# Attention of a three-stage kernel: jobs ordered by a time table per quad of heads, VectorE's small results in a PSUM bank

## The chip, the cores and the metric

The program runs on one core of a Trainium2 chip, in one launch. The metric is the device time in microseconds. The engines are named as in the profile: PE is TensorE (PEld its weight loads), DVE VectorE, ACT ScalarE, POOL GpSimd, SP SyncE, which issues most of the DMAs here (SPq is its queue).

## The reference

Three stages follow each other. The first is attention with a window of 32 positions to either side plus 32 global tokens, for 4 batches of 8 heads of size 64 (512 local, 32 global positions). The second sends each of the 2304 tokens to the one expert out of 8 with the largest logit. The third is an MLP of width 2048.

```python
s_g = scale * np.matmul(q_g, k_all.transpose(0, 1, 3, 2))   # global queries see all 544 keys
out_g = np.matmul(sm(s_g), v_all)
...
mask = np.abs(pos[:, None] - pos[None, :]) <= window
s_ll = np.where(mask, s_ll, -1000000000.0)
s_l = np.concatenate([s_lg, s_ll], axis=-1)
out_l = np.matmul(sm(s_l), np.concatenate([v_g, v_l], axis=2))
...
expert_idx = np.argmax(x @ w_gate, axis=1)      # top-1 MoE, x: 2304 x 512
out[mask] = gate_w[mask, None] * (np.maximum(xe @ w1[e], 0.0) @ w2[e])
...
g = np.where(h >= 1, h, np.where(h <= -1, 0.0, (h + 1) ** 2 / 4))   # h = x @ w_in
return g @ w_out
```

## The kernel before

The 32 heads (4 batches of 8) are 16 **pairs** c, and two pairs are a **quad** q, so a batch is two quads. Each job of the attention is a function that writes its instructions on several engines at once; every engine then runs its own queue in the order in which the jobs were called. The jobs, with the short names that the texts use:

- **S** (`s_pair(c)`): scores of a pair, 64 small matmuls on PE (L253) and two mask matmuls for each head (L256) into two PSUM tiles `sp`.
- **M** (`s_max(n)`): per head, DVE takes the maximum over `sp` (L262, result `mx`, 128x4) and scales it (L263, `mn`). **E** (`s_exp(n)`): four exponentials on ACT (L280) from `sp` to `p`, with their sums.
- **T** (`t_head(n)`): per head, four transposes on PE (L335) into `ps_o`, which DVE copies to `pto` (L336).
- **P** (`pv(c)`): 64 matmuls of `pto` with the values (L380) into `xo`; DVE adds 1e-9 to the sums (L383), takes reciprocals (L384, `ri`) and scales `xo` to `xr` (L385). **V**: POOL spreads a value tile over the partitions in three copies (`spread_v`, L225 to L227), and SP issues the load of a later one (`load_v`).
- **X** (`x_turn`): transposes of `xr` on PE (L395), copied to `xT` by ACT (L396). **XS**: the store of `xr`. **K**: loads of a later pair's keys and queries.
- **G, GM, GE, GN, TG, PG**: the same steps for the 32 global queries of the four heads of a quad (L292; L303 to L305; L316; L322 to L324; L346; L356, whose results POOL copies into `xrg`, L362).
- **L, LT, R** per batch: the router's logits (L402), their transposes (L411), and `route`, nine steps on DVE (L457 to L466) with one exponential on ACT; after it `early` puts the rank matmuls on PE (L491 to L494, into the bank `gxb`), six DVE steps (`place`) and one-hot tiles on POOL.

A list, `units`, holds eight quads of five units (one global, four heads). A loop walks it and calls, at each unit, the jobs that are due at fixed lags: transposes two units after the scores (`LT`), the global transposes three after (`LG`). Jobs of the router go into the lists `tasks` and `fill`, from which the loop calls one task at each unit and up to `RATE` = 8 DVE steps in a row. The last jobs (from `t_head(30)` on) are written out by hand. All loads and stores go through `dma`, which lets a transfer start only when at most `ROOM` = 3.0 units (of 512 KB) are ahead of it on the SP queue.

PSUM has eight banks of 512 fp32 columns: tag "s" 3 (score tiles), tag "x" 1 (`xo`), tag "to" 3 (`ps_o`, `ps_x`, `lg`), and `gxb` alone. Columns 0 to 64 of `gxb` hold a part of the global scores, 128 to 192 the output of PG, 256 to 304 the ranks, 448 to 456 global logits. Where two engines use the same bank, the later one waits for the earlier, whichever columns each uses.

After the attention come the experts and the second MLP, large matmuls over blocks of gathered tokens; the change does not touch them.

## Time and profile before

| | |
|---|---|
| median of 3 runs (lowest, highest) | 740.49 us (738.86, 744.5) |
| profiled execution: its time, its span | 741.64 us, 739.8 us |
| PE busy | 711.3 us (96%), 6609 matmuls |
| DVE, ACT, POOL busy | 486.1 us (66%), 332.1 us (45%), 150.2 us (20%) |
| chain that ended last, by engine | PE 79%, issue 8%, DVE 7%, ACT 2%, DMA 2% |

The span runs from the first to the last instruction that the profiler saw; 1.84 us of the execution lie outside it. The page also cuts the span into 40 slices of 18.5 us and gives each a digit, the busy share of the engine in tenths. PE has 6889888 in the first seven slices, which are the attention, and 9 in every slice from there to the last but one.

### The profile page before, as it was taken

The numbers are of one execution on the slowest core, as the hardware profiler recorded it, in microseconds if no ns is written. First come the engines' busy times: TensorE is split into PE (matmuls) and PEld (weight loads), VectorE is DVE, ScalarE is ACT, GpSimd is POOL, SyncE is SP. The second block draws the span as 40 slices with busy tenths as digits, with TensorE's granted clock in tenths as the row PEclk, the third lists the DMA queues.
The fourth block names the chain that finished last, engine by engine and source line by source line (L and its number), as shares of the span: only waits on it lengthen the run. The fifth ranks groups of instructions, "written<-read, shape, count | busy, mean of one in ns | idle before, by whom it ended". The sixth has DMA issues, their size and how long they took to land.

```text
span 739.8 us, 16419 instructions
## 1 busy us (share of the span) xinstructions
PE 711.3 (96%) x6609; PEld 637.6 (86%) x6609; DVE 486.1 (66%) x887; ACT 332.1 (45%) x762; POOL 150.2 (20%) x185
## 2 busy tenths in 40 slices
PE   6889888999999999999999999999999999999995
PEld 4666666999999999899998898999989898998984
DVE  4778885674516478875777678758775876645443
ACT  4757664453525457664564543233323332322220
POOL 3445543677641340000000000000000000011112
PEclk9999999999999999999999999999999999999998
DMA  8786666485658578763531321101110100001111
GB/s 280 237 258 202 203 194 186 134 291 196 190 166 301 199 252 305 244 208 104 122 99 58 105 68 57 58 1 58 57 58 1 58 0 1 1 30 57 43 43 71
DMA packets 52254, 96.07 MB, mean 130 GB/s; under 512 B 9817, under 2 KB 27769, under 8 KB 50128
## 3 DMA queue, kind: packets, MB, share of 16 engines
q1 hardware_dynamic: 48704, 84.75, 36.1%
q0 software_dynamic: 3472, 10.25, 4.2%
q8 instruction: 53, 0.87, 0.5%
q14 instruction: 25, 0.20, 0.1%
HBM read 80.28 MB, written 14.75 MB: 128 GB/s over the span
## 4 chain that ended last, share of the span: by engine, by line
PE 79%; issue 8%; DVE 7%; ACT 2%; DMA 2%; POOL 1%; SPq 0%; POOLq 0%; ACTq 0%; DVEq 0%
PE fh L988 7%; PE fh L986 7%; PE fh L987 7%; PE o L988 6%; PE o L987 6%; PE o L986 6%; PE hp L988 4%; PE hp L986 4%; PE hp L987 4%; PE yp L986 4%; PE yp L987 4%; PE yp L988 4%; PE ps_o L335 2%; PE sp L253 2%; DMA ks<-in_k 2%
## 5 line engine op out<-in xcount | busy, mean ns | idle before, releaser
L1318 DVE SCALAR_TENSOR_TENSOR r<-r 128x384 f32<-128x384 f32 (+1 forms) x96 | 51.4, 535 | 113.4 <-ACT r L1317 113.4
L986 PE MATMUL o<-wh,gh 128*128 128x512 f32 x272 | 106.9, 393 | 0.8 <-ACT acc L1367 0.8
L988 PE MATMUL o<-wh,gl 128*128 128x512 f32 x272 | 107.6, 396 | 0.0
L987 PE MATMUL o<-wl,gh 128*128 128x512 f32 x272 | 107.3, 394 | 0.0
L1371 POOL DMA_INDIRECT out_dram<-acc,rid x17 | 16.5, 969 | 446.4 <-DVE acc L1369 444.8
L1320 ACT ACTIVATE gh<-g 128x384 fp32r<-128x384 f32 (+1 forms) x96 | 48.8, 508 | 129.2 <-DVE g L1319 129.2
L988 PE MATMUL fh<-yh,wl 128*128 128x384 f32 (+1 forms) x320 | 104.3, 326 | 0.0
L986 PE MATMUL fh<-yh,wh 128*128 128x384 f32 (+1 forms) x320 | 104.2, 326 | 0.0
L987 PE MATMUL fh<-yl,wh 128*128 128x384 f32 (+1 forms) x320 | 104.2, 326 | 0.0
L1317 ACT ACTIVATE r<-fh,half 128x384 f32<-128x384 f32 (+1 forms) x96 | 54.0, 562 | 105.6 <-PE fh L988 105.0
L986 PEld LDWEIGHTS fh<-yh,wh 128*128 128x128 f32 x320 | 60.2, 188 | 3.5
L987 PEld LDWEIGHTS fh<-yl,wh 128*128 128x128 f32 x320 | 60.2, 188 | 3.4
L988 PEld LDWEIGHTS o<-wh,gl 128*128 128x128 f32 x272 | 51.1, 188 | 12.4 <-DVE gl L1326 0.4
L988 PEld LDWEIGHTS fh<-yh,wl 128*128 128x128 f32 x320 | 60.2, 188 | 0.0
L986 PEld LDWEIGHTS o<-wh,gh 128*128 128x128 f32 x272 | 51.1, 188 | 9.1 <-ACT acc L1367 1.2
L987 PEld LDWEIGHTS o<-wl,gh 128*128 128x128 f32 x272 | 51.1, 188 | 8.1
L280 ACT ACTIVATE p<-sp,mn 128x128 f32<-128x128 f32 x128 | 45.2, 373 | 20.0 <-DVE mn L263 10.1
L1319 DVE TENSOR_TENSOR g<-r,fh 128x384 f32<-128x384 f32 (+1 forms) x96 | 51.0, 532 | 3.3
L986 PE MATMUL yp<-hTh,w2h 128*128 128x256 f32 (+5 forms) x176 | 51.7, 294 | 0.0
L988 PE MATMUL yp<-hTh,w2l 128*128 128x256 f32 (+5 forms) x176 | 51.2, 291 | 0.0
L987 PE MATMUL yp<-hTl,w2h 128*128 128x256 f32 (+5 forms) x176 | 51.1, 290 | 0.0
L1326 DVE TENSOR_TENSOR gl<-g,gh 128x384 fp32r<-128x384 f32 (+1 forms) x96 | 50.7, 529 | 0.0
(238 smaller groups left out, 1617.3 us busy)
## 6 DMA issues: line engine op xcount, KB each, us to landing
w1r<-in_w SPq DMA_DIRECT2D x32, 512.0 KB
w2r<-in_w SPq DMA_DIRECT2D x32, 512.0 KB
wraw<-in_wf SPq DMA_DIRECT2D x16, 1024.0 KB
ks<-in_k SPq DMA_DIRECT2D x16, 400.0 KB
v<-in_v SPq DMA_DIRECT2D x16, 384.0 KB
yr<-ys SPq DMA_DIRECT2D x68, 64.0 KB
qp<-in_q SPq DMA_DIRECT2D x16, 256.0 KB
xs<-xr SPq DMA_DIRECT2D x8, 512.0 KB
```

The costliest lines, as they stand in the source:

```text
L253: nc.tensor.matmul(sps[2 * c + z][a * WIN:(a + 1) * WIN, i, :], lhsT=q[r, j * WIN:(j + 1) * WIN], rhs=k_at(k, r, j), start=(i == 0), stop= ...
L280: nc.scalar.activation(p[:, i, :].rearrange("p (a b w) -> p a b w", a=2, b=2), v, AF.Exp, bias=mn[:, i:i + 1], scale=scale, accum_out=ss[b ...
L335: nc.tensor.transpose(o[:, i, :], p[:, i, :], ident)
L986: nc.tensor.matmul(o, lhsT=ah, rhs=bh, start=first, stop=False)
L987: nc.tensor.matmul(o, lhsT=ah, rhs=bl, start=False, stop=False)
L988: nc.tensor.matmul(o, lhsT=al, rhs=bh, start=False, stop=last)
L1317: nc.scalar.activation(r[:, 0:w], o[:, 0:w], AF.Relu, bias=half, scale=0.5)
L1318: nc.vector.scalar_tensor_tensor(r[:, 0:w], r[:, 0:w], 1.0, r[:, 0:w], ALU.min, ALU.mult)
L1319: nc.vector.tensor_tensor(g[:, 0:w], r[:, 0:w], o[:, 0:w], ALU.max)
L1320: nc.scalar.activation(gh[:, 0:w], g[:, 0:w], AF.Copy)
L1326: nc.vector.tensor_tensor(gl[:, 0:w], g[:, 0:w], gh[:, 0:w].bitcast(F32), ALU.subtract)
L1371: w = nc.gpsimd.indirect_dma_start(out=out, out_offset=bass.IndirectOffsetOnAxis(ap=rid[:, tt:tt + 1].bitcast(U32), axis=0), in_=a, in_off ...
```

## The change

**The order.** The loop with its lags goes. Each job has a time, in units of one quad: the quad's number plus a number from `TIMES` (one for each time that the job occurs in a quad) plus, for the global jobs of the first two quads, a number from `SHIFT`. All jobs are sorted by that time and called in that order. The jobs of the end that are in `LAST` are left to the part written out by hand, in which one transpose of `xr` is now called later and POOL's `weigh` as well.

**The small results.** `mx` (M), the sums plus 1e-9 (P), and for the first three batches the logits `L` and the scores `sc` (`route`) are no tiles in SBUF any more but columns 64 to 72, 72 to 80, 192 to 224 and 80 to 120 of `gxb`. The instructions are the same ones.

**The banks.** The bank of tag "x" goes to tag "s", which has 4; `xo` is taken from tag "to", which keeps 3.

**The start.** The load of `qg` (the queries of the global tokens) is issued ahead of the first values.

In the changed file the lines up to P's stand one lower (L262 is L261, L335 is L334); those of `route` are unchanged.

```diff
@@ -180,7 +180,7 @@
...
-    wps = ps.tile([128, 512], F32, tag="s", name="sp", bufs=3)
+    wps = ps.tile([128, 512], F32, tag="s", name="sp", bufs=4)
...
@@ -244,8 +244,7 @@
     def s_pair(c):
...
         for z in range(2):
-            home, n = ("x", 1) if c == 1 and z else ("s", 3)
-            sps[2 * c + z] = ps.tile([128, 4, BW], F32, tag=home, name="sp", bufs=n)
+            sps[2 * c + z] = ps.tile([128, 4, BW], F32, tag="s", name="sp", bufs=4)
...
@@ -257,7 +256,7 @@
 
     def s_max(n):
         sp = sps[n]
-        mx = ap.tile([128, 4], F32, tag="mx4", name="mx4", bufs=2)
+        mx = gxb[:, 64 + 4 * (n % 2):68 + 4 * (n % 2)]
         mn = ap.tile([128, 4], F32, tag="mn", name="mn", bufs=3)
         nc.vector.tensor_reduce(mx, sp, axis=AX.X, op=ALU.max)
         nc.vector.tensor_single_scalar(mn, mx, -scale, op=ALU.mult)
...
@@ -372,7 +371,7 @@
...
-        xo = ps.tile([128, 4, 2, D], F32, tag="s" if c == 15 else "x", name="xo", bufs=3 if c == 15 else 1)
+        xo = ps.tile([128, 4, 2, D], F32, tag="to", name="xo", bufs=3)
...
@@ -380,8 +379,9 @@
...
-        nc.vector.tensor_scalar_add(r, ss[b][:, :, 2 * g:2 * g + 2], 1e-9)
-        nc.vector.reciprocal(r, r)
+        e = gxb[:, 72:80].rearrange("p (i z) -> p i z", i=4)
+        nc.vector.tensor_scalar_add(e, ss[b][:, :, 2 * g:2 * g + 2], 1e-9)
+        nc.vector.reciprocal(r, e)
...
@@ -447,9 +447,9 @@
     def route(b):
...
-        L = ap.tile([128, 5, 8], F32, tag="L", name="L", bufs=2)[:, 0:nt] if b < B - 1 else L4
+        L = gxb[:, 192:224].rearrange("p (t e) -> p t e", e=E) if b < B - 1 else L4
...
-        sc = ap.tile([128, 5, 8], F32, tag="sc", name="sc", bufs=2)[:, 0:nt]
+        sc = gxb[:, 80:80 + nt * E].rearrange("p (t e) -> p t e", e=E)
...
@@ -594,15 +594,6 @@
...
-    units = []
-    for q in range(8):
-        units += [("g", q), ("h", 4 * q), ("h", 4 * q + 1), ("h", 4 * q + 2), ("h", 4 * q + 3)]
...
@@ -614,8 +605,8 @@
...
     load_q(1)
+    nc.sync.dma_start(qg, d["qg"])
     load_v(0)
-    nc.sync.dma_start(qg, d["qg"])
...
@@ -632,84 +623,61 @@
...
-    pend_n, pend_g, pend_v = [], [], []
-    LT, LG = 2, 3
-    nv = 3
-    for s in range(len(units)):
-        kind, a = units[s]
-        tk, ta = units[s - LT] if s >= LT else (None, None)
-        if tk == "h":
-            t_head(ta)
...
-        if kind == "h":
-            if a % 2 == 0 and a != 2:
-                s_pair(a // 2)
...
+
+    def values(c):
+        if c + 3 < 16:
+            load_v(c + 3)
+        if 0 < c < 14:
+            spread_v(c + 2)
+
+    def ahead(c):
+        if c + 4 < 16:
+            load_k(c + 4)
+        if c + 3 < 16:
+            load_q(c + 3)
...
-        if kind == "h" and a % 2 == 1:
-            if a // 2 + 4 < 16:
-                load_k(a // 2 + 4)
-            if a // 2 + 3 < 16:
-                load_q(a // 2 + 3)
...
-        for c in pend_v:
-            pv(c)
-            if nv < 16:
-                load_v(nv)
-                nv += 1
-            if 0 < c < 14:
-                spread_v(c + 2)
-            b, g = divmod(c, 4)
-            if g % 2:
-                tasks.append(lambda b=b, g=g: x_store(b, g // 2))
-            tasks.append(lambda b=b, g=g: x_turn(b, g))
-            if b < B - 1 and g == 3:
-                then = [lambda b=b: tasks.append(lambda: early(b))]
-                tasks += [lambda b=b: logits(b), lambda b=b: logits_t(b),
-                          lambda b=b, then=then: fill.extend(route(b) + then)]
...
-        if tk == "h" and ta % 2 == 1:
-            pend_v.append(ta // 2)
...
-        if kind == "h":
-            s_rest(RATE)
-        for _ in range([7, 5, 3, 1].count(len(units) - s)):
-            raw.pop(0)()
-    weigh(xz, 128, nc.gpsimd)
+
+    def routed(b):
+        fill.extend(route(b) + [lambda: tasks.append(lambda: early(b))])
+
+    def work(_):
...
+
+    def weight(k):
+        raw.pop(0)()
+
+    JOBS = {"G": s_glob, "GM": g_max, "GE": g_exp, "GN": g_norm, "TG": t_glob, "PG": pv_glob, "S": s_pair, "M": s_max, "E": s_exp,
+            "T": t_head, "P": pv, "V": values, "X": lambda c: x_turn(*divmod(c, 4)), "XS": lambda h: x_store(*divmod(h, 2)), "K": ahead,
+            "F": work, "Z": later, "L": logits, "LT": logits_t, "R": routed, "W": weight}
+    TIMES = {"G": (-0.01,), "GM": (0.051,), "GE": (0.219,), "GN": (0.481,), "TG": (0.505,), "PG": (0.761,), "S": (0.233, 0.574,), "M": (0.259, 0.387, 0.683, 0.797,), "E": (0.358, 0.636, 0.817, 1.058,), "T": (0.755, 0.861, 1.216, 1.219,), "P": (1.099, 1.472,), "V": (1.191, 1.63,), "X": (1.278, 1.7,), "XS": (1.991,), "K": (0.685, 1.489,), "F": (0.252, 0.681, 0.177, 0.898,), "Z": (0.598, 0.159, 0.495, 0.715, 1.027,), "L": (2.825,), "LT": (3.094,), "R": (3.103,)}
...
+    WEIGHTS = (7.629, 6.164, 8.624, 7.969)
+    LAST = {("T", 30), ("T", 31), ("P", 14), ("P", 15), ("X", 13), ("X", 14), ("X", 15), ("XS", 7)}
+    plan = []
+    for nm, when in TIMES.items():
+        per = len(when)
+        for n in range(per * 8 if nm not in ("L", "LT", "R") else B - 1):
+            q, k = divmod(n, per) if nm not in ("L", "LT", "R") else (2 * n, 0)
+            plan.append((q + when[k] + SHIFT.get((nm, n), 0.0), nm, n))
+    plan += [(t, "W", n) for n, t in enumerate(WEIGHTS)]
+    for t, nm, n in sorted(plan):
+        if (nm, n) not in LAST:
+            JOBS[nm](n)
     t_head(30)
     pv(14)
     t_head(31)
-    for t in tasks:
-        t()
+    s_rest(99)
+    later(0)
+    s_rest(99)
+    later(0)
+    assert not fill and not tasks
+    weigh(xz, 128, nc.gpsimd)
+    x_turn(B - 1, 1)
     dma(xs[B * SL:N, 0:DM], xrg)
```

What the order of instructions is on the engines shows best at three places.

PE, the first instructions after the warm-up matmuls, before: the scores of pair 0 and pair 1 (`sp<-ks,qp` with their masks), two heads' transposes, then G of quad 0 (`sp<-ks,qg`).

```order
L253 MATMUL sp<-ks,qp 32x128 x32
L256 LDWEIGHTS mask
L256 MATMUL sp<-mask 128x4x96
L256 LDWEIGHTS mask
L256 MATMUL sp<-mask 128x4x96
L253 MATMUL sp<-ks,qp 32x128 x32
L256 LDWEIGHTS mask
L256 MATMUL sp<-mask 128x4x96
L256 LDWEIGHTS mask
L256 MATMUL sp<-mask 128x4x96
L335 MATMUL ps_o<-ident,p 128x128 x8
L292 MATMUL sp<-ks,qg 32x320 x4
```

The same place after:

```order
L291 MATMUL sp<-ks,qg 32x320 x4
L291 MATMUL sp<-ks,qg 32x160 x4
L291 MATMUL gxb<-ks,qg 32x64 x4
L252 MATMUL sp<-ks,qp 32x128 x32
L255 LDWEIGHTS mask
L255 MATMUL sp<-mask 128x4x96
L255 LDWEIGHTS mask
L255 MATMUL sp<-mask 128x4x96
L252 MATMUL sp<-ks,qp 32x128 x32
```

G of quad 0, which needs `qg` and the keys of pairs 0 and 1, moved from behind both pairs' scores to the front of them.

DVE, the last of the router's eight steps in a row for the first batch (from L461 on) and what follows, before:

```order
L461 SCALAR_TENSOR_TENSOR sc<-L,cst 128x32
L462 TENSOR_REDUCE m_1047<-sc 128x4
L463 TENSOR_TENSOR oh<-sc,m_1047 128x32
L464 TENSOR_REDUCE se<-ex 128x4
L465 TENSOR_SCALAR se<-se 128x4
L262 TENSOR_REDUCE mx_1179<-sp 128x4
L263 TENSOR_SCALAR mn<-mx_1179 128x4
L383 TENSOR_SCALAR ri<-ss 128x8
L384 RECIPROCAL ri<-ri 128x8
L385 TENSOR_TENSOR xr<-xo,ri 128x4x128
L466 RECIPROCAL gid<-se 128x4
L336 COPY pto<-ps_o 128x512
```

The same place after:

```order
L460 TENSOR_TENSOR gxb<-gxb,mx 128x32
L461 SCALAR_TENSOR_TENSOR gxb<-gxb,cst 128x32
L462 TENSOR_REDUCE m_1066<-gxb 128x4
L463 TENSOR_TENSOR oh<-gxb,m_1066 128x32
L464 TENSOR_REDUCE se<-ex 128x4
L465 TENSOR_SCALAR se<-se 128x4
L335 COPY pto<-ps_o 128x512 x2
L466 RECIPROCAL gid<-se 128x4
L261 TENSOR_REDUCE gxb<-sp 128x4
L262 TENSOR_SCALAR mn<-gxb 128x4
```

The steps still stand in a row, but two copies of transposes (`pto<-ps_o`) now come right behind them, where two maxima, P's three steps and the last router step stood ahead of the first copy.

PE at the same place, from the output matmuls of a pair to the first rank matmul (`gxb<-ohs,ones`), before:

```order
L380 MATMUL xo<-v,pto 32x64 x32
L335 MATMUL ps_o<-ident,p 128x128 x4
L346 MATMUL ps_o<-ident,pgz_130 128x128 x6
L253 MATMUL sp<-ks,qp 32x128 x32
L256 LDWEIGHTS mask
L256 MATMUL sp<-mask 128x4x96
L256 LDWEIGHTS mask
L256 MATMUL sp<-mask 128x4x96
L395 MATMUL ps_x<-ident,xr 128x128 x4
L335 MATMUL ps_o<-ident,p 128x128 x4
L491 LDWEIGHTS ones
L491 MATMUL gxb<-ohs,ones 128x32
```

The same place after:

```order
L334 MATMUL ps_o<-ident,p 128x128 x8
L252 MATMUL sp<-ks,qp 32x128 x32
L255 LDWEIGHTS mask
L255 MATMUL sp<-mask 128x4x96
L255 LDWEIGHTS mask
L255 MATMUL sp<-mask 128x4x96
L395 MATMUL ps_x<-ident,xr 128x128 x4
L379 MATMUL xo<-v,pto 32x64 x32
L491 LDWEIGHTS ones
L491 MATMUL gxb<-ohs,ones 128x32
```

Two heads' transposes now stand ahead of the scores instead of one, the global transposes (L346) are gone from there to behind the ranks, and the pair's output matmuls (`xo<-v,pto`) stand between the transposes of `xr` and the ranks.

## Rows read from the trace of the kernel before

The names and lines are those of the section on the kernel; a busy time in a window counts only what lies in it.

**Rows 1.** Windows: each engine's busy time in seven stretches, with clock and DMA

```profile
core 0: us, PE busy (x) PEld busy (x) DVE busy (x) ACT busy (x) POOL busy (x), PEclk, DMA share, GB/s
10.00:20.00 10.00, 7.83 (x183) 5.87 (x181) 8.07 (x20) 5.58 (x29) 5.96 (x9) 1.00 0.97 306
25.43:111.22 85.79, 75.96 (x2164) 56.07 (x2163) 70.10 (x197) 55.35 (x252) 41.07 (x72) 0.97 0.74 221
50.00:60.00 10.00, 7.85 (x208) 6.00 (x207) 9.00 (x26) 6.55 (x30) 4.50 (x6) 0.93 0.67 214
60.00:70.00 10.00, 9.93 (x287) 6.89 (x288) 8.51 (x28) 5.93 (x30) 6.29 (x11) 0.90 0.76 227
...
110.00:120.00 10.00, 8.31 (x268) 6.30 (x269) 7.26 (x30) 5.81 (x31) 5.03 (x10) 0.84 0.55 159
111.22:128.00 16.78, 14.21 (x379) 11.34 (x379) 8.76 (x31) 8.01 (x32) 6.79 (x10) 0.94 0.56 172
136.00:400.00 264.00, 263.44 (x1809) 252.26 (x1808) 168.34 (x216) 139.38 (x214) 73.31 (x59) 1.00 0.61 196
```

**Rows 2.** Timeline of PE, 48 to 128 us, start and length, idle time before in brackets

```profile
49.22 0.45 PE L253 MATMUL sp<-ks,qp 64*32 64x128 f32 x15 [1.93 <-issue]
...
51.57 1.37 PE L335 MATMUL ps_o<-ident,p 128*128 128x128 f32 x4
...
57.21 0.66 PE L395 MATMUL ps_x<-ident,xr 128*128 128x128 f32 x4 [2.09 <-DVE pto L336]
57.70 0.60 PE L335 MATMUL ps_o<-ident,p 128*128 128x128 f32 x4
...
86.08 0.66 PE L395 MATMUL ps_x<-ident,xr 128*128 128x128 f32 x4 [1.90 <-DVE pto L336]
...
109.96 1.33 PE L335 MATMUL ps_o<-ident,p 128*128 128x128 f32 x4 [1.85 <-DVE pto L336]
...
116.04 0.91 PE L380 MATMUL xo<-v,pto 128*32 128x64 f32 x49 [1.41 <-issue]
...
122.39 0.99 PE L380 MATMUL xo<-v,pto 128*32 128x64 f32 x56 [0.88 <-DVE pto L336]
```

**Rows 3.** Sources: shortest, median and longest of four DVE lines in the attention

```profile
L263 DVE TENSOR_SCALAR mn<-mx x30: 169/170/821, 12.0 to 115.1; 128x4 f32<-128x4 f32 x30
...
L383 DVE TENSOR_SCALAR ri<-ss x16: 157/163/819, 15.2 to 122.3; 128x8 f32<-128x8 f32 x16
...
L336 DVE COPY pto<-ps_o x31: 653/681/693, 12.2 to 121.7; 128x512 f32<-128x512 f32 x31
...
L304 DVE TENSOR_REDUCE mg<-gxb x8: 213/214/215, 14.2 to 101.0; 128x1 f32<-128x64 f32 x8
```

**Rows 4.** Timeline of DVE around the router's steps of the first and third batch

```profile
51.95 0.81 DVE L460 TENSOR_TENSOR L<-L,mx 128x32 f32<-128x32 f32 x1
...
53.79 0.50 DVE L463 TENSOR_TENSOR oh<-sc,m 128x32 bf16<-128x32 f32 x1
...
56.49 0.66 DVE L336 COPY pto<-ps_o 128x512 f32<-128x512 f32 x1
...
106.55 0.19 DVE L460 TENSOR_TENSOR L<-L,mx 128x32 f32<-128x32 f32 x1
```

**Rows 5.** Timeline of POOL, 49 to 56 us

```profile
51.89 0.82 POOL L225 COPY v<-v 96x768 f32<-96x768 f32 x1 [3.35 <-DMA v<-in_v]
```

**Rows 6.** Timeline of PE, the first scores and outputs

```profile
4.80 1.15 PE L253 MATMUL sp<-ks,qp 64*32 64x128 f32 x64 [0.16 <-DMA qp<-in_q]
...
8.63 1.15 PE L253 MATMUL sp<-ks,qp 64*32 64x128 f32 x64 [2.25 <-DMA qp<-in_q]
...
15.46 1.21 PE L380 MATMUL xo<-v,pto 128*32 128x64 f32 x64 [1.18 <-DMA ks<-in_k]
```

**Rows 7.** Timeline of SP's queue at the start

```profile
5.30 0.42 SPq L618 DMA_DIRECT2D qg<-in_qg  x1
```

**Rows 8.** Timeline of POOL at the start

```profile
9.92 0.82 POOL L225 COPY v<-v 96x768 f32<-96x768 f32 x1 [7.58 <-DMA v<-in_v]
```

**Rows 9.** Waits, 12 to 130 us: total, times, longest

```profile
POOL v L225 <- DMA v<-in_v: 34.2, 12, 4.5
...
PE gxb L356 <- DVE mg L304: 0.9, 1, 0.9
```

More of the change, by code (lines that the diff above doesn't have):

```diff
@@ L283, in s_glob @@
     def s_glob(q):
-        sp = ps.tile([128, 512], F32, tag="s", name="sp", bufs=3)
+        sp = ps.tile([128, 512], F32, tag="s", name="sp", bufs=4)
         for part in range(3):
@@ L568, in zsteps @@
         for g in range(2):
-            o = ps.tile([128, 4, 128], F32, tag="x" if g else "s", name="zh", bufs=1 if g else 3)
+            o = ps.tile([128, 4, 128], F32, tag="s", name="zh", bufs=4)
             for u in range(4):
@@ L634, in emit, with later @@
         spread_v(c)
[L635 removed]
     moved.clear()
[L637 to L654 removed]
+    def values(c):
[8 more added lines that the diff above has]
+            load_q(c + 3)
+    def later(_):
         while tasks:
@@ L692, in emit @@
-        for q in pend_n:
-            g_norm(q)
-        pend_n, pend_g, pend_v = [], [q for q in pend_g if gq == ("g", q)], []
-        if tk == "h" and ta % 2 == 1:
-            pend_v.append(ta // 2)
-        if kind == "h" and a != 3:
-            s_exp(a)
-        elif kind == "g":
-            g_exp(a)
-            pend_n.append(a)
-        if kind == "h":
-            s_rest(RATE)
-        for _ in range([7, 5, 3, 1].count(len(units) - s)):
-            raw.pop(0)()
-    assert not fill, len(fill)
```

30 lines of the change are left out of this document (2 added, 28 removed).

## The prediction

> **What bounds the kernel now.** I read the page's slices first: from the eighth on PE is busy all the time, and the window over the experts agrees, 263.44 of 264 us [rows 1]. The change leaves that part alone, so all it can give lies in the attention, before 128 us. There the windows say that no engine is full: between the fourth pair's scores and the last pair's (25.43 to 111.22) PE works 75.96 of 85.79 us, DVE 70.10, ACT 55.35, and in the tail (to 128) PE 14.21 of 16.78. PE idles 9.83 + 2.57 = 12.40 us. The timeline of PE says where, and on whom it waits.
>
> Three gaps of 2.09, 1.90 and 1.85 us wait for DVE's copy `pto` [rows 2], one in each batch that is routed in the loop. The timeline of DVE shows why: the router's steps stand in a row ahead of that copy, and some of them are long. The step L460 takes 0.81 us in the first batch and 0.19 in the third [rows 4]; the long one runs beside a POOL copy that began at 51.89 and took 0.82 [rows 5]. The sources show the same of other small steps that work on SBUF: L263 has 170 ns as its median and 821 at most, L383 163 and 819. Operations that read PSUM, the copy L336 (653 to 693) and the maximum L304 (213 to 215), are never stretched [rows 3]. So VectorE's small steps wait for POOL's copies while they work on SBUF, and PE pays for it at the next copy.
>
> The rest is smaller. Some transposes go at the pace at which ACT delivers the exponentials of their head: four take 1.37 us at 51.57 and 0.60 at 57.70 [rows 2]. There are five of the long kind in the stretch. And the granted clock falls below 1.00 after gaps: 0.93 and 0.90 in the two windows from 50 to 70, 0.84 from 110 to 120 [rows 1], a mixture of the levels of 2.4 and 1.2 GHz.
>
> **The change part by part.** All sums go against the profiled execution (741.64 us, 1.84 outside its span), and the difference is then taken off the median, 740.49, which is 1.15 lower.
>
> *Start.* PE now begins with G of quad 0, which needs `qg` and the keys of pair 1. The first scores began at 4.80, and those of pair 1 waited 2.25 us for `qp`, to 8.63 [rows 6]. `qg` is issued behind that `qp`; its 256 KB at 306 GB/s, the rate of the window 10 to 20 [rows 1], are 0.84 us, so G starts near 9.5, 4.7 later than PE's first work did. The 2.25 are swallowed by the new wait, and the 1.18 before the first outputs at 15.46 [rows 6], a wait for keys, probably too. 4.7 - 2.25 - 1.18 = **+1.3**. If nothing is given back it is +4.7; if the one wait of G's maximum on PG (0.9, [rows 9]) goes as well, +0.4. The values behind `qg` come 0.84 later than POOL's 9.92 [rows 8]; the outputs need them at 15.46, so that hides. Ahead of the change `qg` was issued at 5.30 [rows 7].
>
> *Gaps behind the router.* In the order, two copies now follow right behind the router's steps, and PE has eight transposes, scores and outputs to do ahead of the ranks. With `L` and `sc` in PSUM the steps should take about 0.2 as at 106.55. All three gaps go: 2.09 + 1.90 + 1.85 = **-5.8**. Next in line is then DVE itself: 70.10 us of work in a stretch of some 77, so small waits will stay.
>
> *Paced transposes.* 5 x (1.37 - 0.60) = 3.85. The table puts T 0.16 to 0.40 quads behind its E; a quad is some 13 us (85.79 for six, less the gain), so that is 2 us or more, longer than the 1.37 of a whole paced group. I take four of five: **-3.1**.
>
> *Clock.* 10 x (0.07 + 0.10 + 0.16) = 3.3 us were lost. Each fall stands by a gap that goes, but a PE that idles to 9.5 may begin at the lower level, and other gaps may come. **-2.5**; ends 0 and -3.3.
>
> *Small results in `gxb`.* The same instructions on other addresses. New are orderings between engines in that bank: G's matmuls into it wait for the last `mn` on DVE, PG's as well, and the ranks for a reciprocal of P: 8 + 8 + 3 = 19 places. Behind each of them PE's transposes, scores and outputs are queued; behind DVE's maxima, which wait for ACT's GE in turn, the exponentials. The trace has one case: eight PG groups already share the bank with DVE's L304, and one waited, for 0.9 us [rows 9]. Ends: 19 x 0.9 = 17.1, and 19 x 0.9/8 = 2.1. I take 0.14 each, **+2.6**, near the lower end, since the matmuls of the row and of the new places both come some us behind the DVE work they wait for.
>
> *Tail.* The waits of 1.41 and 0.88 at 116.04 and 122.39 [rows 2] come from the order there. P of pair 13 (1.1) moves ahead of the last scores, X of pair 13 and POOL's `weigh` move later; their sum of work is the same, and a transpose of 0.60 fits into either gap. Half of 2.29: **-1.1**, ends 0 and -2.3.
>
> *At nothing:* the banks (`xo` now shares three with the transposes; a fourth score tile lets S run ahead; PE orders itself, and DVE's copies free them), the loads (the same bytes for each quad, see the second rival), the four early expert weights (issued in quads 6 to 8, needed behind 128).
>
> Sum: +1.3 - 5.8 - 3.1 - 2.5 + 2.6 - 1.1 = -8.6, so 740.49 - 8.6 = **731.9**.
>
> **The rivals.**
>
> *One bank ties three engines together (slower).* If each of the 19 places waits 0.9 as the one in the rows did, they cost 17.1 in place of 2.6: -8.6 + 14.5 = +5.9, 746.4. It decides from 0.14 + 8.6/19 = 0.59 us each. Against it: seven of eight PG groups did not wait. The row shows a wait between different columns of one bank (PG writes 128 to 192, L304 reads 0 to 64). The Trainium skill, "PSUM — Partial Sum Buffer", section "PSUM bank collisions raise a hardware error", says why these waits can't be dropped: two engines must be kept apart by bank and quadrant, not by address. By that rule the row's wait is what every new place may cost. Chance 0.08.
>
> *Loads come late.* 221 GB/s x 85.79 + 172 x 16.78 are 21.8 MB; in 10 us less that is 236 GB/s in place of 213, where 306 was seen at a share of 0.97 [rows 1]. In the mean there is room, but POOL already waited 34.2 us in 12 waits for values [rows 9], 2.9 each, and PG now reads a value tile 0.57 quads (7 us) after its load is issued. If each of the six middle quads loses 1 us: -2.6, 737.9. Chance 0.17.
>
> *It doesn't do what it says.* The router's steps are still eight in a row; if they hold the copies up as before, the 5.8 stay: -2.8, 737.7. Chance 0.14.
>
> *Every small step is dearer on PSUM.* L304 takes 213 ns on 64 columns of PSUM, L263 170 on 4 of SBUF: at most 43 ns for some 114 moved accesses, 4.9 us of DVE; half on the path, +2.5: 734.4. The widths explain much of the 43. The Trainium skill, "Perfetto Trace Analysis", section "Optimizing Scalar/DVE Operations", gives an overhead of about 60 ns for DVE on SBUF and 125 on PSUM; by an estimate from that page, 114 x 65 ns are 7.4 us, half of it +3.7. Chance 0.07.
>
> *PE without waits.* All idle time in the loop and tail, 12.40, the pacing and the clock go: 12.40 + 3.85 + 3.3 = 19.6, less 1.3 and 2.1: -16.2, 724.3. Speaks for it that DVE loses its stretched steps as well. Chance 0.16.
>
> **How the numbers follow.** The forecast has 0.38 and by itself reaches from 728 to 736. The range leaves out the slower rival and the end of the fastest: 724 to 739.5. One per cent (7.4 us) is about what a measurement here can tell from no change. Faster than 733.1: two thirds of the forecast, the last rival, a little of the others, 0.50; slower than 747.9: the upper part of the first rival and a start at its worst end, 0.06; between: 0.44.
>
> **What would show it.** In the profile after: PE's first matmul near 9.5 and pair 3's scores about 1.3 later; no gap over 1 us ahead of transposes behind the router; L262 (once L263) with a maximum near its median; clock 1.00 between the batches; PE's waits on `gxb` below 3 us in sum; the attention's end near 119 (128 less 8.6). Wrong it would be by waits for values ahead of PG or P, waits of G or PG on `mn`, or a low clock in the first 20 us.

## The result and the profile after

The changed kernel takes 752.41 us in the median of 4 runs (745.71 to 753.23), the kernel before 741.0. The ratio is 1.0111, 95% interval 1.0069 to 1.0153: slower, by about 8 us by the ratio; the medians and the two profiled executions (753.08 against 741.64) are 11.4 us apart. From the end of the attention on the profiled executions are alike (611.7 us of span against 611.8), so all of their difference lies in the attention. All ratios here compare undisturbed runs, and the profile of e14_order_bank, which is of a disturbed one, is not used.

PE's timeline of the changed kernel, at the places that the prediction named:

```profile
9.25 1.82 PE L291 MATMUL sp<-ks,qg 64*32 64x320 f32 x16 [4.62 <-DMA v<-in_v]
...
16.02 1.14 PE L252 MATMUL sp<-ks,qp 64*32 64x128 f32 x62 [1.73 <-ACT p L279]
...
26.91 0.88 PE L355 MATMUL gxb<-v,pgt 128*32 128x64 f32 x48 [1.46 <-DVE mn L262]
...
34.15 0.86 PE L291 MATMUL sp<-ks,qg 64*32 64x320 f32 x8 [1.96 <-DMA ks<-in_k]
...
38.79 1.16 PE L252 MATMUL sp<-ks,qp 64*32 64x128 f32 x64
...
59.94 0.19 PE L491 MATMUL gxb<-ohs,ones 128*128 128x32 bf16 x1 [1.14 <-DVE ri L384]
...
89.12 0.19 PE L491 MATMUL gxb<-ohs,ones 128*128 128x32 bf16 x1 [1.33 <-DVE ri L384]
...
118.52 1.16 PE L252 MATMUL sp<-ks,qp 64*32 64x128 f32 x64
...
123.61 0.48 PE L334 MATMUL ps_o<-ident,p 128*128 128x128 f32 x1 [3.17 <-issue]
...
138.97 0.53 PE L432 MATMUL lg<-ident,lgt 96*128 96x96 f32 x4
```

The gaps of 2 us for the copies `pto` [rows 2] have no counterpart any more. Others stand in their place. PE begins at 9.25 (the wait of 4.62 is named after the values; the load that G needs, `qg`, is issued just ahead of them). Pair 1's scores, which waited for `qp` up to 8.63 [rows 6], are finished from 16.02 on (62 of the 64 matmuls): they wait for an exponential that must free a score bank, since G of quad 0 has taken one of the four. PG waits 1.46 for `mn`, G of quad 2 waits 1.96 for keys, the ranks wait 1.14 and 1.33 for P's reciprocal, and the longest gap, 3.17 at 123.61, waits for nothing that the trace knows. The fifth pair's scores start at 38.79 (32.7 before), the last pair's at 118.52 (111.22), and the last logits are transposed at 138.97 (127.5).

The windows, to be read beside [rows 1]:

```profile
core 0: us, PE busy (x) PEld busy (x) DVE busy (x) ACT busy (x) POOL busy (x), PEclk, DMA share, GB/s
0.00:10.00 10.00, 4.18 (x17) 1.56 (x21) 0.28 (x2) 1.49 (x2) 1.79 (x8) 0.87 0.82 255
10.00:20.00 10.00, 7.77 (x184) 4.92 (x176) 5.10 (x13) 5.38 (x30) 5.75 (x8) 0.79 0.95 287
20.00:30.00 10.00, 8.52 (x334) 6.73 (x334) 7.03 (x21) 6.97 (x35) 2.71 (x10) 1.00 0.19 62
30.00:40.00 10.00, 8.04 (x175) 6.15 (x174) 6.39 (x17) 4.84 (x24) 4.49 (x6) 0.83 0.84 275
120.00:130.00 10.00, 5.71 (x109) 4.36 (x111) 4.66 (x16) 3.68 (x20) 4.80 (x9) 0.67 0.51 173
```

The granted clock is 0.87 and 0.79 in the first 20 us, 0.83 from 30 to 40 and 0.67 from 120 to 130: part of the time at 1.2 GHz in place of 2.4, each time behind one of the gaps above (4.62 and 1.73, 1.96, 3.17 us). From 20 to 30 the transfers run at a share of 0.19.

VectorE's small steps, as sources (shortest, median, longest in ns), answer to [rows 3] and [rows 4]:

```profile
L262 DVE TENSOR_SCALAR mn<-gxb x32: 161/163/164, 14.2 to 126.8; 128x4 f32<-128x4 f32 x32
...
L383 DVE TENSOR_SCALAR gxb<-ss x16: 154/162/171, 20.8 to 133.4; 128x8 f32<-128x8 f32 x16
...
L460 DVE TENSOR_TENSOR gxb<-gxb,mx x3: 199/199/200, 54.9 to 112.5; 128x32 f32<-128x32 f32 x3
```

L262 is the old L263: 164 ns at most, where it had 821. L460 takes 199 in every batch. That part came as forecast, and this step is not dearer on PSUM (163 in the median, 170 on SBUF). 23 of its 32 runs here lie beside an instruction of POOL and take no longer for it; in the kernel before 21 do, and every run of it over 172 ns is one of these.

PE's waits from 12 to 140 us (total, times, longest), six of the groups:

```profile
PE gxb L355 <- DVE mn L262: 2.8, 2, 1.5
PE gxb L491 <- DVE ri L384: 2.5, 2, 1.3
...
PE sp L252 <- issue: 3.6, 4, 1.8
PE ps_o L334 <- issue: 3.2, 1, 3.2
...
PE xo L379 <- issue: 1.9, 4, 1.1
...
PE ps_x L395 <- issue: 1.6, 1, 1.6
```

PE's waits for the bank's other users are 5.8 us in all groups together (the third group is G's, 0.5), and those called issue 10.3, where the kernel before had 1.1 and 3.3. "Issue" is time in which PE waits for nothing that the profile shows.

### The profile page after: what moved, and what is told of

Same layout as the page of the kernel before. It is cut to its first block, busy times and chain, and to the rows that moved or that the text cites. A ratio compares the mean times of both kernels' runs of the same rounds, so it can differ in the third digit from the quotient of the medians.

```text
span 751.2 us, 16418 instructions
## 1 busy us (share of the span) xinstructions
PE 714.1 (95%) x6609; PEld 639.5 (85%) x6609; DVE 480.6 (64%) x887; ACT 331.9 (44%) x762; POOL 149.4 (20%) x185
## 4 chain that ended last, share of the span: by engine, by line
PE 66%; issue 7%; DVE 3%; POOL 1%; ACT 1%; POOLq 0%; ACTq 0%; DVEq 0%
PE fh L956 7%; PE fh L954 7%; PE fh L955 7%; PE o L956 6%; PE o L955 6%; PE o L954 6%; PE hp L956 4%; PE hp L954 4%; PE hp L955 4%; PE yp L954 4%; PE yp L956 4%; PE yp L955 4%; POOL out_dram L1339 1%; PE xTp L909 1%; DVE g L1287 1%
## 5 line engine op out<-in xcount | busy, mean ns | idle before, releaser
L1286 DVE SCALAR_TENSOR_TENSOR r<-r 128x384 f32<-128x384 f32 (+1 forms) x96 | 51.4, 536 | 113.3 <-ACT r L1285 113.2
```

What stands on the lines that cost most here:

```text
L1286: nc.vector.scalar_tensor_tensor(r[:, 0:w], r[:, 0:w], 1.0, r[:, 0:w], ALU.min, ALU.mult)
```

## The experiments

First the numbers of all runs. Starts and the end of the attention are from PE's timeline of one profiled execution; "issue" is the sum of PE's waits of this kind from 12 to 140 us, "gxb" that of its waits ahead of matmuls into this bank, without those for loads, for `pgt` and for issue; the ratio is that to the kernel before in the same runs. One profiled execution is one draw: that of the changed kernel is the second longest of four (745.71 to 753.23), that of e8_keys (746.26) lies below the median of its runs, 749.1.

| kernel | pair 4 | pair 15 | end | issue | gxb | ratio (95%) |
|---|---|---|---|---|---|---|
| before | 32.7 | 111.2 | 128.0 | 3.3 | 1.1 | 1 |
| after | 38.8 | 118.5 | 139.5 | 10.3 | 5.8 | 1.0111 (1.0069 to 1.0153) |
| e1_start | 36.2 | 118.1 | 134.4 | 6.4 | 7.6 | 1.0078 (1.0039 to 1.0118) |
| e2_sbuf | 38.5 | 115.3 | 132.5 | 5.6 | 0.2 | 1.0080 (1.0043 to 1.0116) |
| e3_room | 37.8 | 125.5 | 142.4 | 3.6 | 7.6 | 1.0192 (1.0130 to 1.0253) |
| e4_before_bank | 34.3 | 115.3 | 133.8 | 2.1 | 8.7 | 1.0101 (1.0059 to 1.0142) |
| e5_order | 31.9 | 110.6 | 127.3 | 10.0 | 1.0 | 0.9997 (0.9960 to 1.0034) |
| e6_before_route | 34.6 | 111.5 | 128.3 | 3.2 | 1.1 | 1.0011 (0.9971 to 1.0051) |
| e7_before_mx | 32.4 | 113.8 | 130.9 | 1.7 | 8.4 | 1.0074 (1.0039 to 1.0109) |
| e8_keys | 36.0 | 116.4 | 132.8 | 5.9 | 7.6 | 1.0086 (1.0040 to 1.0132) |
| e9_order_route | 32.5 | 109.2 | 127.3 | 6.4 | 1.4 | 0.9986 (0.9967 to 1.0006) |
| e10_order_room2 | 34.2 | 121.8 | 140.6 | 6.3 | 1.5 | 1.0199 (1.0176 to 1.0223) |
| e11_order_room4 | 31.4 | 112.5 | 129.4 | 8.1 | 1.0 | 1.0048 (1.0027 to 1.0069) |
| e12_before_loads | 33.6 | 108.4 | 124.5 | 4.5 | 1.1 | 0.9967 (0.9946 to 0.9988) |
| e13_shift | 34.8 | 109.7 | 127.2 | 5.7 | 1.0 | 1.0109 (1.0074 to 1.0145) |
| e14_order_bank | | | | | | 1.0034 (1.0001 to 1.0067) |
| e15_order_late | 35.2 | 113.2 | 132.1 | 7.6 | 0.2 | 1.0031 (0.9999 to 1.0062) |
| e16_best | 33.6 | 110.5 | 127.8 | 9.2 | 1.0 | 1.0022 (0.9993 to 1.0051) |
| e17_before_shift | 37.0 | 116.1 | 132.0 | 9.8 | 1.1 | 1.0094 (1.0059 to 1.0129) |
| e18_order_shift | 33.3 | 112.1 | 129.0 | 9.1 | 1.0 | 1.0022 (0.9998 to 1.0045) |

**The start and the bank, each undone.** e1_start:

```diff
-    nc.sync.dma_start(qg, d["qg"])
     load_v(0)
+    nc.sync.dma_start(qg, d["qg"])
...
-    SHIFT = {("G", 0): -0.168, ("GM", 0): 0.478, ("GE", 0): 0.495, ("GN", 0): 0.518, ("G", 1): -0.116, ("GM", 1): 0.159, ("GE", 1): 0.248, ("GN", 1): 0.125, ("TG", 0): 0.542, ("PG", 0): 0.628, ("TG", 1): 0.779, ("PG", 1): 0.639}
+    SHIFT = {("G", 0): 0.872, ("GM", 0): 0.812, ("GE", 0): 0.646, ("GN", 0): 0.518, ("G", 1): 0.3, ("GM", 1): 0.255, ("GE", 1): 0.248, ("GN", 1): 0.125, ("TG", 0): 0.542, ("PG", 0): 0.628, ("TG", 1): 0.779, ("PG", 1): 0.639}
```

> The changed kernel with the start of the one before: the first values are loaded ahead of qg, the scores of pairs 0 and 1 stand ahead of G of quad 0, and G of quad 1 stands behind the scores of pair 2; all other times of the table stay. The pair scores of the changed kernel were 3.2 us late at the fourth pair and 6.1 late at the fifth, of 11.4 in all. If the start is the main loss (late first work, then the low clock and loads that are late in turn), the fifth pair's scores come at 33 to 34 us and the time falls by 5 to 7, to about 746. If the order and the bank lose the time anyway and the start only shifts where, the fifth pair is early but the end is not, and the time stays within 2 of 752.

e2_sbuf puts back the four tiles (the removed lines of the diff on `mx`, `e`, `L` and `sc`).

> The changed kernel with mx, the sums plus 1e-9, L and sc back in SBUF tiles; order, banks and start stay. In the changed kernel PE waited 5.8 us for the bank's other users (2.8 ahead of PG for mn, 2.5 ahead of the ranks for P's reciprocal, 0.5 ahead of G). If the shared bank is the loss, these waits go and the time falls by 4 to 6, to 747. If the bank gave more at DVE than it cost at PE, the small steps on SBUF are stretched by POOL's copies again (L262 up to 0.8 us), and the time is the same or up to 4 us longer.

Each brings back about a third of a per cent, which is inside the intervals and less than was expected of a main loss. With the start undone the fifth pair still begins at 36.2, not at 33 to 34: something else is late there. With the bank undone its waits are gone (0.2 in place of 5.8) and the attention of the profiled execution ends 7 us earlier, but its experts lose 5 us again (616.6 us from there to the end), with issue waits in them that the changed kernel's experts do not have, and in the ratio 2 us are left. The largest of these waits:

```profile
PE yp L953 <- issue: 2.3, 2, 1.2
```

**The bank in the order of before.** e4_before_bank makes the four edits on `mx`, `e`, `L` and `sc` of the diff in the kernel before; e7_before_mx has the one on `mx` alone, e6_before_route those on `L` and `sc`.

> The kernel before with the small results alone moved to the bank gxb (mx, the sums plus 1e-9, L, sc); its order, banks and start stay. If the bank frees VectorE from POOL's copies, L263, L383, L460 and L461 are no longer stretched, the three gaps of 2.09, 1.90 and 1.85 us shrink to about 1 each, and the time falls by 3 to 5, to 737. If the bank's orderings cost more than that, PE waits for mn ahead of G and PG, and the time is 741 to 746.

Its waits of PE:

```profile
PE gxb L356 <- DVE mn L263: 4.7, 5, 1.5
PE ps_x L396 <- DVE pto L336: 2.1, 2, 1.8
PE gxb L356 <- ACT p L280: 1.9, 1, 1.9
```

The copies (`pto`) hold PE less, 2.9 us in all in place of 6.9, and L263 is never over 163 ns. But PG now waits for `mn` five times, nearly 1 us each, and once 1.9 us for an exponential. The sum is a loss of 1.0 per cent. Two runs divide it:

> The kernel before with the maxima mx alone in the bank. In e4_before_bank PE waited 4.7 us ahead of PG for mn, 0.8 ahead of the ranks, and the time rose by about 7. If that is the wait that the bank adds, this kernel keeps it, without the shorter router steps: 6 to 9 us slower than the kernel before. If the cost lay with P's sums or the router's tiles, it is within 2 us of the kernel before.

> The kernel before with the router's logits L and scores sc alone in the bank; the maxima and P's sums stay in SBUF. The ranks that follow on PE need the router's result anyway, so the bank adds no wait to them. If the orderings of mn with G and PG are what the bank costs, this has none of them, keeps the short router steps (0.2 us in place of 0.5 to 0.8) and is 1 to 4 us faster than the kernel before. If any use of the bank by VectorE costs, it is slower by 2 or more.

The maxima alone keep these waits (4.7 us for `mn` in five places, 2.0 for the exponential) and cost 0.74 per cent. The router's tiles alone have none of them and are equal to the kernel before, where 1 to 4 us less was expected. So most of the price is that of one ordering: PG, and behind it the whole of PE's queue, may not start before DVE's last `mn`, which has nothing to do with PG but sits in the same bank. P's sums alone were not run.

e6_before_route also tests the reading of the three gaps behind the router:

```profile
L460 DVE TENSOR_TENSOR gxb<-gxb,mx x3: 199/200/200, 52.1 to 106.7; 128x32 f32<-128x32 f32 x3
```

```profile
PE ps_o L335 <- DVE pto L336: 2.2, 2, 2.0
PE ps_x L395 <- DVE pto L336: 2.0, 2, 1.1
```

L460 is as short as in the changed kernel, yet PE waits 4.8 us for copies in all, where it waited 6.9. In the third batch, whose router steps were short already, the step stretched ahead of the copy is L263 (0.82 us before, 0.71 here). But short steps alone do not close the gaps: 2.9 us are left with all four results in the bank (e4_before_bank), but only 1.3 in the new order with none of them in it (e5_order, below).

**The queue of SP.** Here stand the rows of the changed kernel's SP queue that explain the idle transfers from 20 to 30, and the same place with K of pairs 1 and 3 put ahead of V of pairs 0 and 2 (two entries more in the table of shifts, e8_keys):

```diff
+    SHIFT.update({("K", 1): -0.309, ("K", 3): -0.309})
```

> The changed kernel with one edit of its table: K of pairs 1 and 3 stand ahead of V of pairs 0 and 2. In the changed kernel SP stood still for 10.3 us (17.5 to 27.9) with the load of the fourth values, whose tile PG of quad 0 frees, and the keys behind it came late: G of quad 2 waited 1.96 for them at 34.15, and the clock fell. If the SP queue is that cause, the keys are issued near 17.5, the fifth pair's scores come 2 to 4 us earlier (35 to 37), and the time is 748 to 750. If the queue only waits because the compute is late, nothing moves: 751 to 753.

After:

```profile
17.18 0.33 SPq L194 DMA_DIRECT2D qp<-in_q  x1
27.85 1.27 SPq L194 DMA_DIRECT2D v<-in_v  x3
29.22 0.37 SPq L194 DMA_DIRECT2D ks<-in_k  x1
```

The SP queue's own waits, 14 to 36 us:

```profile
SPq L194 <- PE gxb L355: 10.3, 1, 10.3
```

e8_keys:

```profile
18.15 0.33 SPq L194 DMA_DIRECT2D ks<-in_k  x1
...
28.56 1.78 SPq L194 DMA_DIRECT2D v<-in_v  x4
```

In the changed kernel SP issues nothing for 10 us: the load of the fourth values waits for PG of quad 0 to free its tile, and PG of quad 0 stands late in the table. The keys behind it go out at 29.22. Put ahead, they go out at 18.15 though the values still wait to 28.56, the fifth pair starts 2.8 us earlier, and no wait of PE for loads is left. The ratio falls from 1.0111 to 1.0086, which alone is inside the error.

**The order alone, and the start alone.** e5_order joins the edits of e1_start, e2_sbuf and e8_keys; what is left of the change is the order in the loop and the tags. e15_order_late is e5_order without the edits of e1_start, e14_order_bank without those of e2_sbuf.

> The order of the loop alone: the changed kernel with the small results back in SBUF, with the start of the kernel before (as in e1_start), and with the second and fourth keys' loads (K of pairs 1 and 3) put ahead of the first and third values' (V of pairs 0 and 2) on the SP queue. In e2_sbuf the way from the fifth pair's scores to the last pair's was 76.9 us, 78.5 in the kernel before. If the order itself is sound and only its start, its SP queue and the bank lose, the time is that of the kernel before or 1 to 4 us less (738 to 742). If the order loses by itself, it stays at 745 or more.

> e5_order with the changed kernel's start (G of quad 0 first, qg ahead of the first values), the keys still ahead of the values and the small results in SBUF. It differs from e2_sbuf by the SP queue alone and from e5_order by the start alone. If the start by itself costs, it is 3 to 5 us above e5_order, with the first matmul behind the warm-up near 9.5 us and the fourth pair's scores 2 to 4 us later. If the loss of e2_sbuf (0.8 per cent) was the SP queue's, it is within 2 us of e5_order.

> e5_order with all four small results in the bank, as the changed kernel has them. In the order of before the bank cost 0.74 per cent (e7_before_mx) to 1.01 (e4_before_bank). If it costs as much in the new order, this is 4 to 7 us slower than e5_order, with 5 to 8 us of PE waits on gxb ahead of PG and the ranks. If the new order has places for these waits, or they only take the place of issue waits, it is within 2 us of e5_order, with fewer issue waits.

e5_order equals the kernel before. So the three sets of edits together hold the whole loss: 1.0111 against 0.9997 is 1.14 per cent, with an error of 0.56 (the root of the sum of the squares of both intervals, as below), some 8 us. How it divides is less sure. From e5_order the start alone costs 0.34 per cent (2.5 us, error 0.49) and the bank alone 0.37 (2.7 us, error 0.50): neither is clear of zero. The SP queue is put at 0.49 by e2_sbuf against e15_order_late (error 0.48) and at 0.25 by the changed kernel against e8_keys (error 0.62). The first of these is not only the queue's: in the profiled executions the two end the attention within 0.4 us of each other (132.5 and 132.1), and e2_sbuf loses its 5 us in the experts, where e15_order_late has no issue wait.

**Where the order's gain went.** Some of PE's waits in e5_order:

```profile
PE xo L379 <- issue: 4.2, 3, 1.9
PE sp L252 <- issue: 3.7, 4, 1.2
...
PE ps_x L394 <- issue: 1.6, 1, 1.6
...
PE xo L379 <- DVE pto L335: 1.3, 2, 0.9
```

The gaps for `pto` are 1.3 us (6.9 before), and those called issue are 10.0 (3.3 before). That is 5.6 us won and 6.7 lost. The rest also shifts: 1.9 for exponentials and 1.2 for keys are gone, 2.8 ahead of TG of quad 0 and some small ones are new. The first theory was that PE's instructions, which are read by DMA in packets of 16 KB, queue behind the loads. Four runs bear on it:

```diff
-    ROOM = 3.0
+    ROOM = 2.0
```

(in the changed kernel, e3_room, and in e5_order, e10_order_room2; 4.0 in e11_order_room4.) e12_before_loads, the kernel before with:

```diff
+        if s in (12, 17, 22, 27):
+            k = (s - 12) // 5
+            dma(w1r[k], d["w1"][0, k * 128:(k + 1) * 128, :])
         for _ in range([7, 5, 3, 1].count(len(units) - s)):
             raw.pop(0)()
```

> The changed kernel with ROOM 2.0 in place of 3.0, so that less is queued ahead of any transfer. PE had 10.3 us of waits that the profile calls issue, 3.3 in the kernel before; each ends some 2 to 3 us after one 16 KB instruction packet lands, and they lie where loads fill the engines. If the instructions of PE queue behind the loads, these waits shrink by half or more, and unless the loads themselves come late the time falls by 3 to 5, to 748. If the issue waits have nothing to do with the loads, they stay at 8 to 12 us and the time is the same or longer by late loads.

> e5_order with ROOM 2.0. In e5_order PE's waits for others are small, but those that the profile calls issue are 10.0 us (3.3 in the kernel before). If PE's instructions queue behind loads, fewer loads in flight bring them to 3 to 6 us, as e3_room did for the changed kernel (10.3 to 3.6), and late loads appear in their place; the time is 739 to 747 by which of the two is larger. If they come from PE running through its instructions with fewer pauses, whatever the loads, they stay at 9 to 11 us and the time does not fall.

> e5_order with ROOM 4.0, the other side of e10_order_room2. If PE's instructions queue behind loads, the issue waits grow from 10.0 to 12 or more and the time rises by 2 or more. If they do not, the waits stay at 9 to 11 and the time is the same within 2, since e5_order shows no wait for loads.

> The kernel before with four loads of 512 KB more (the four early expert weights, loaded a first time in quads 2 to 5 and again where they were; the data are the same). If loads delay PE's instructions, the issue waits grow from 3.3 us to 6 or more and PE's gaps for copies stay; the time rises by 3 to 6. If issue waits do not depend on the loads, they stay at 3 to 4 and the time rises only if loads of the attention come late (waits for ks, qp or v appear).

With ROOM 2 the issue waits fell, 10.3 to 3.6 and 10.0 to 6.3, but with ROOM 4 they did not rise (8.1, at a time half a per cent longer), and four more loads of 512 KB in the kernel before left them at 4.5 and the time a little shorter. So the amount of loads in flight is not shown to set their sum; the theory falls in that form. What is left of it is taken up below. (ROOM 2 itself costs 2 per cent against before, by late loads: 9.0 us of PE's waits in e10_order_room2. Why e12_before_loads is 0.3 per cent faster is not settled; its clock is 1.00 in every 20 us.)

The places of the waits follow a count. These windows reach from 0 to just before four issue waits of e5_order, with PE's and PEld's instructions so far in brackets:

```profile
0.00:58.90 58.90, 47.78 (x1361) 34.23 (x1362) 38.91 (x113) 37.15 (x170) 26.56 (x55) 1.00 0.80 246
0.00:62.88 62.88, 50.87 (x1488) 36.79 (x1489) 41.31 (x119) 38.44 (x176) 29.63 (x59) 1.00 0.80 244
0.00:68.05 68.05, 54.83 (x1615) 39.77 (x1615) 44.49 (x129) 42.28 (x194) 31.89 (x62) 1.00 0.80 244
0.00:96.70 96.70, 80.51 (x2376) 58.75 (x2377) 68.17 (x198) 61.27 (x281) 45.79 (x86) 1.00 0.79 241
```

1361 + 1362 = 2723, and likewise 2977, 3230 and 4753: distances of 254, 253 and 6 x 253.8. The same counts come back in every kernel, but for seven short waits (2.2 us in sum over all traces) that stand elsewhere (the kernel before waits at 2216 and 5512, the changed one at 1708, 2216, 2723, 2977, 3230, 4496, 4750, 5004, 5257 and 5512). Three runs moved the program against the counts by narrow matmuls at the start:

```diff
     for _ in range(9):
         nc.tensor.matmul(wps, lhsT=warm[:, 0:128], rhs=warm, start=True, stop=True)
+    for _ in range(64):
+        nc.tensor.matmul(wps[:, 0:4], lhsT=warm[:, 0:128], rhs=warm[:, 0:4], start=True, stop=True)
```

(this is e17_before_shift; e18_order_shift has 32 of them, e13_shift 70 and only three of the nine wide ones.)

> e5_order with six of the nine warm-up matmuls replaced by 70 narrow ones (4 columns), so that every later PE instruction stands 128 places further on in PE's queue. In all kernels so far the issue waits lie at distances of 253 to 255 PE instructions or multiples of it (in e5_order at counts 947, 1707, 2723, 2977, 3230, 4753, 5261, 5515, and one off the grid at 5776), whatever job stands there, and one 16 KB instruction packet is read for each such block. If PE waits for the next block of its instructions, the waits stay at these counts within 15 and so move to other jobs, 128 instructions earlier in the program; their sum may be anything from 4 to 11 us and the time moves with it, 738 to 745. If the jobs at these places are the cause, the waits keep their jobs and stand at counts 128 higher.

> The kernel before with 64 narrow warm-up matmuls (4 columns) more ahead of its first scores: nothing else changes, but every later PE instruction stands 128 places further on in PE's queue. They take about 2 us in which PE waits for loads anyway (the second pair's queries come at 8.6). In e13_shift such a step cost 1.1 per cent, and its profile shows the loss in the experts (3 us of issue waits and 1.6 more there, a lower clock), with the attention as long as without it. If the place of the blocks of PE's instructions does that, the kernel before pays as well: issue waits in the experts and 4 to 9 us. If e13_shift lost by its fewer warm-up matmuls at full width, this one is within 2 us of the kernel before.

> e9_order_route with 32 narrow warm-up matmuls more, 64 instructions, half the step of e13_shift. If the place of the blocks decides, its issue waits stand at the same counts as in the other kernels, thus in other jobs than in e9_order_route, and the time differs from 0.9986 by anything from -3 to +8 us; if only fewer warm-ups cost, it stays within 2 us.

e13_shift, windows up to three of its waits:

```profile
0.00:54.10 54.10, 44.65 (x1235) 33.72 (x1235) 32.71 (x90) 30.59 (x138) 22.57 (x47) 0.97 0.74 231
0.00:59.13 59.13, 48.96 (x1362) 37.16 (x1363) 36.67 (x105) 35.19 (x160) 24.68 (x50) 0.97 0.76 234
0.00:67.92 67.92, 56.37 (x1615) 42.89 (x1616) 44.03 (x125) 40.45 (x185) 30.85 (x61) 0.97 0.76 235
```

2470, 2725 and 3231: the same counts, in other jobs. Its attention is as long as that of e5_order (127.2 and 127.3 us); it loses in the experts, where it alone of these two has such waits:

```profile
PE yp L955 <- issue: 2.1, 2, 1.6
PE hp L955 <- PEq L1243: 1.6, 1, 1.6
...
PE yp L956 <- issue: 0.8, 1, 0.8
```

In the kernel before, the step of 128 instructions, with nothing changed behind it, gives this:

```profile
20.99 0.63 PE L255 MATMUL sp<-ks,qp 64*32 64x128 f32 x22 [3.22 <-issue]
...
42.18 0.79 PE L382 MATMUL xo<-v,pto 128*32 128x64 f32 x29 [2.01 <-issue]
```

```profile
PE xo L382 <- issue: 4.6, 5, 2.0
PE sp L255 <- issue: 3.9, 3, 3.2
```

The issue waits go from 3.3 to 9.8 us, one of them 3.22 long, at counts 695 and 1708, and the kernel is slower by 0.94 per cent (0.59 to 1.29). That is nearly the size of the whole result. The narrow matmuls themselves are not the cause in the profiled execution: the third pair's scores, ahead of the first long wait, begin 0.3 us later than before (16.88 and 16.61), the fifth pair's 4.3 later. From there to the end of the attention it takes 95.0 us, the kernel before 95.3, though its issue waits there are 6.6 us against 3.3: a larger sum of such waits does not by itself lengthen the time. Its experts lose little (612.9 us against 611.8), where issue waits in them had been expected. The half step, e18_order_shift, moved the waits to other jobs as well (9.1 us, counts 694 to 5768) and cost 0.36 against e9_order_route, with intervals that overlap.

The trace also has the packets themselves. The kernel before reads 53 of them, 16.4 KB each, on the queue of PE's instructions:

```profile
q8 instruction: 53, 0.87, 0.5%
```

In the changed kernel the longest issue wait ends at 123.61, and the count of the wait before it was reached at 116.75. Between the two there is one such packet, from 121.35 to 122.33. Here are the stretch ahead of it and the DMA view of 121.3 to 122.4:

```profile
116.75:121.35 4.60, 3.68 (x128) 2.89 (x127) 3.62 (x17) 3.54 (x18) 1.98 (x4) 1.00 0.91 262
```

```profile
q8 instruction: 1, 0.02, 5.6%
```

It is the same in e17_before_shift, where the packet ahead of the wait of 3.22 runs from 18.46 to 19.56. Over the 19 traces used, 51 issue waits at these counts last 1 us or longer in the attention, and each ends 1.2 to 1.6 us after a packet has landed. So in these waits PE waits for its instructions. In the seven longest (2.2 to 3.2 us) the packet starts 4.1 to 5.6 us after PE passed the count before, where 1.7 us is the median of all crossings, and the DMA engines are about 0.9 to 1.0 busy in between. e11_order_room4 has five packets that start more than 3.5 us after it; the two runs with ROOM 2 and all kernels in the old order at its old place have none. To that extent the theory of the queue fits the longest waits; that the loads are what delays their packets is argued from this, not shown.

The Trainium skill, "Runtime: NRT & Kernel Launch", section "Instruction fetch mechanics", says that an engine's instructions are refilled in blocks of 16 KiB, 256 instructions, fetched ahead, and that crossing a block is mostly hidden. The counts agree with the blocks (253 to 255 of the trace's instructions). Most crossings are hidden here too: at 308 of 425 in the attention of these traces PE has no issue wait. At the others it waits 0.2 to 3.2 us.

**A version that might beat both.** e9_order_route takes e5_order with the router's tiles in the bank, e16_best moves TG of quad 0 behind the next transposes (in SHIFT its 0.542 becomes 0.722).

> e5_order with the router's L and sc in the bank again: the order of the loop, the start of the kernel before, the keys ahead of the values, and of the bank only what e6_before_route had. e5_order was equal to the kernel before (0.9997). In the order the router's steps are followed by two copies that PE waits for little, so if all waits of PE that can go have gone and the instruction supply limits it, this gives nothing: 740 to 744. If DVE's stretched router steps still hold PE up, it is 1 to 3 us faster than e5_order.

> e9_order_route with TG of quad 0 moved from ahead of P of pair 0 to behind the transposes that follow it, since TG waited 2.8 to 3.5 us there. If that wait only covers others, the time is that of e9_order_route (0.9986 of the kernel before); if it was on the path, 1 to 3 us less, 738 to 740, faster than both kernels.

0.9986 and 1.0022: neither differs from the kernel before. The wait of TG (3.5 us in e9_order_route) is gone in e16_best, its issue waits rose from 6.4 to 9.2: it only covered others.

## Why the prediction was wrong

The sum had the order win 12.5 us (gaps -5.8, transposes -3.1, clock -2.5, tail -1.1) and the start and the bank cost 3.9. Measured, the order alone wins nothing (0.9997, e5_order), and the start, the bank and the SP queue cost some 8 us.

*What bounds the kernel now*: the gaps were there, and POOL's copies do stretch the steps, but the stretch was only part of the gaps. In the old order 4.8 of 6.9 us for `pto` stay with short router steps (e6_before_route) and 2.9 with all small steps short (e4_before_bank), in the new order alone 1.3 (e5_order). All three gaps went, so -5.8 is right as a price; but it is the order that closes them more than the bank.

*"Next in line is then DVE itself"* is the step that failed most. Next in line were PE's own instructions: issue waits rose from 3.3 to 10.0 us by the order alone (10.3 in the changed kernel), 6.7 where the gaps gave 5.6. The trace of before showed two such waits, 1.93 at 49.22 and 1.41 at 116.04 [rows 2]; the first was not weighed, the second was put into the tail as a matter of order. By e17_before_shift the kernel before had its blocks at places where their crossing cost little; another order has them elsewhere. The kernels in the new order had 3.6 to 10.3 us of issue waits, those in the old order at its old place 1.7 to 4.5. What the new order would take without these waits was not measured.

*Start*, +1.3 (bounds +0.4 to +4.7), was too small. In the changed kernel pair 3's scores came 3.2 us later, not 1.3, and the fifth pair's 6.1. PE began at 9.25 as forecast, but the sum took the waits of 2.25 and 1.18 as given back; instead pair 1's scores met a new wait for a score bank, and the clock was at 0.87 and 0.79. "The loads, at nothing" overlooked what V is queued ahead of: a load that waits for a tile stops the keys behind it on SP's queue (10.3 us). The start alone measures 2.5 us and the queue 1.9 to 3.6, with the errors given above. The rival of late loads came nearest to it, but it looked for late values in the middle of the loop, not for late keys at its start.

*Small results in the bank*, +2.6 (19 x 0.14 is 2.66), had the right mechanism. In the changed kernel 5 of the 19 places waited (two PG, two ranks, one G), 5.8 us or 0.31 for each of the 19, about twice the 0.14 that the sum took, and the sign "below 3 us in sum" did not come. That the ratio of e14_order_bank gives 2.7 us is luck as far as the record goes, with an error of 3.7. In the old order five PG of eight waited nearly 1 us each, and there the bank lost 5.5 to 7.5 us: the rival's price of 0.9 holds where a place waits, but most places do not. The new waits lie between different columns of one bank, as the one in [rows 9] did. With that the rule of the Trainium skill cited there, "PSUM — Partial Sum Buffer", section "PSUM bank collisions raise a hardware error", agrees.

*Paced transposes*, -3.1: right as a reading. In e5_order and in the changed kernel no four transposes between 45 and 118 us take over 0.66 us, where five groups took some 1.37 before, and the 1.9 us of waits for exponentials are gone.

*Clock*, -2.5: the wrong sign. It did not fall between the batches any more, but in the first 20 us, from 30 to 40 and from 120 on, behind the gaps named above. By the prediction's own sum these four windows are 10 x (0.13 + 0.21 + 0.17 + 0.33) = 8.4 us against 3.3, an upper bound, since PE idles in part of them.

*Tail*, -1.1: from the last pair's scores to the end 16.8 us before, 16.7 in e5_order: nothing. In the changed kernel it is 21.0, with one issue wait of 3.17 and the low clock behind it.

That each small step is dearer on PSUM, a rival, fell: 163 ns against 170 for the same step of 128x4. The figures of 60 and 125 ns from the Trainium skill, "Perfetto Trace Analysis", section "Optimizing Scalar/DVE Operations", do not show here.

Open stays what lets one packet start 4 us late and another at once, whether the loads or something else, and how much of 1.0111 would be left with the blocks at a better place.

## What to carry to other kernels

Before gaps on the bound engine are summed up as a gain, look at what the engine meets when it no longer pauses: here the waits that the profile calls issue were the sign that its instruction stream was next, and the count of its instructions and the packets of its instruction queue told where. A reordering moves these places; a step of 64 or 128 idle instructions at the start tells how much of a difference of 1 per cent may be the place and not the order. A job's load belongs, with all that stands behind it on its queue, to the time at which its buffer comes free; and a free corner of a PSUM bank is not free if another engine's queue passes through that bank.
